# An attention and MLP kernel in float16: 20 more identity matmuls in two waits of TensorE in the first batch

## The chip, the cores and the metric

The kernel runs on one core of one Trainium2 chip. A core has five engines with a queue of instructions each: TensorE (PE, whose weight loads are shown as PEld), VectorE (DVE), ScalarE (ACT), GpSimd (POOL) and SyncE (SP). They run side by side and wait for each other on semaphores. DMA transfers are issued by SP, ACT and POOL and carried out by 16 DMA engines. The metric is the time of one execution in microseconds (us) on the device, taken as the median of several runs.

## The reference

Two layers, one after the other. The first is attention of 12 heads over 448 tokens with a head size of 64, for a batch of 8, with a normalisation of q and k. The second is an MLP of 768 to 3072 to 768 with a normalisation ahead of it and a sum behind.

```python
def rmsnorm(x, g):
    return x / np.sqrt(np.mean(x * x, axis=-1, keepdims=True) + 1e-06) * g
q_n, k_n = rmsnorm(q, g_q), rmsnorm(k, g_k)                 # [8, 12, 448, 64]
scores = 1.0 / np.sqrt(64) * np.matmul(q_n, k_n.transpose(0, 1, 3, 2))
attn = np.exp(scores - np.max(scores, axis=-1, keepdims=True))
attn = attn / (np.sum(attn, axis=-1, keepdims=True) + 1e-09)
x = np.matmul(attn, v).transpose(0, 2, 1, 3).reshape(8, 448, 768)
mu, var = mean and variance of x over the last axis
xn = (x - mu) / np.sqrt(var + 1e-06) * g_ln
out = x + np.maximum(xn @ w_ch1, 0.0) @ w_ch2               # float32
```

The identity matmuls that this case is about are no part of it: nothing reads what they write.

## The kernel before

**How the work is cut.** The heads are taken in pairs, six for each batch, 48 in all. A pair's tokens are seven groups of 128 rows. Pairs are prepared in units of one or two. The MLP of a batch runs while the attention of the next batch is worked on, piece by piece between its matmuls. The last batch's MLP has nothing beside it.

**The order is written out by hand.** Every engine runs its instructions in the order in which the program emits them. For the first batch the list `ORDER` (L39 to L50) gives that order, token by token, and `first_attention` (L502) turns each token into instructions. Those that matter here:

- `Sp.i`: the scores of pair p, group i (L406), one or two matmuls of 448 columns on PE (L417, or L427 and L428 for the left group 6), then an exponential on ACT (L433).
- `Kp`, `Qp`: the transposes of k and q of a pair on PE (L377, L380, L397), with a copy from PSUM behind them: k by DVE (L385), q by ACT for the pairs in `ACT_Q` (0, 2, 4, 5; L400) and otherwise by DVE (L402).
- `mu`: the second copy of q in float16 that the transposes read (L336), for unit 1 on DVE.
- `Vp.i`: exponentials times v (L470, L472).
- `Hn`: n matmuls of the 128 x 128 identity with itself into a PSUM bank of their own, psW, which nothing reads (L541 to L544). Each is one weight load and one matmul.
- `Jn`: the same as transposes, into an unused part of the bank for transposes (L547).
- `Ln`: the loads of a unit of q, k, v by SP (L149, L157).

In the list, `Q0` (transposes of q of the first pair) is followed, with entries for other engines between, by `S0.0`; and `S0.6` is followed by `Q1`.

**The end.** In the last batch the second group of MLP rows ends as follows. PE computes the products of L832, the last of them in two halves of 192 columns. DVE adds each to the sums (L768). SP and ACT store the rows as they are done: L967 for tokens of a batch (tile x), L970 for the left tokens (tile xl), where for each 64 rows of xl SP issues one store and ACT the other. Behind the last product PE runs `END_WORK`, 44 more identity matmuls into psW (L1003). Then each engine loads a flag (L1232) and jumps by it (L1233): a general path, a long piece of program for inputs out of range, is passed over. Behind the jump SP waits for all stores, and the engines meet (L1260).

The few lines of the end that a sentence doesn't say:

```python
for c in range(0, HCOL, 192):
    for s in range(4):
        yield half / 4, lambda s=s, c=c: product(f"4{c}", A2(hi), T4, s, c=slice(c, c + 192))
    yield 0, lambda c=c: self.add(b, t0 + 1, 0, bank[f"4{c}"][:, c:c + 192], c, c + 192)
    yield 0, lambda c=c: self.store(b, t0 + 1, slice(c, c + 192), nc.scalar)
```

Of the kernel before, what the change touches and what calls it, by code (L numbers as in the profile page):

```python
# [36 lines left out]


ORDER = """  # L39
b0 H12 a0 L4 c0 i0 e0 j0 H24 b1 gq0 d0 k0 l0 a1 m0 K0 G gk0 i1 H10 L5 c1 Q0 d1 j1 S0.0 b2 S0.1  # L40
H5 a2 e1 g1 S0.2 c2 S0.3 k1 l1 z0 d2 e2 m1 K1 S0.4 i2 H16 S0.5 S0.6 Q1 g2 H5 J8 b3 l2 j2 k2 c3
V0.0 S1.0 z2 S1.1 S1.2 V1.0 J8 a3 m2 H4 V0.1 z3 S1.3 K2 S1.4 V0.2 Q2 V0.3 V0.4 d3 S1.5 V0.5 V0.6
S2.0 S1.6 V1.1 V1.2 S2.1 e3 W0 i3 K3 V2.0 S2.2 V2.1 S2.3 Q3 j3 T0 S2.4 k3 V1.3 g3 V1.4 S2.5 S2.6
l3 b4 V1.5 m3 c4 S3.0 S3.1 V2.2 S3.2 K4 a4 V1.6 S3.3 V2.3 S3.4 Q4 d4 V2.4 V2.5 V3.0 V3.1 V3.2
V2.6 i4 S3.5 j4 J4 S3.6 V3.3 T1 K5 e4 k4 S4.0 W1 S4.1 S4.2 Q5 z4 b5 S4.3 V3.4 V4.0 V3.5 S4.4
V4.1 V4.2 S4.5 W2 V4.3 S5.0 g4 V3.6 S4.6 S5.1 J4 V5.0 V4.4 G2 S5.2 l4 T3 K6 V4.5 V5.1 V4.6 S5.3
T4 V5.2 a5 L6 V5.3 S5.4 m4 Q6 i5 S5.5 V5.4 S5.6 V5.5 V5.6 T5 S6.0 S6.1 J4 S6.2 A V6.0 S6.3 V6.1
N0 N1 S6.4 S6.5 J4 V6.2 X0 V6.3 d5 j5 N2 S6.6 V6.4 X1 z5 Q7 c5 V6.5 R U0 e5 U1 g5 X2 V6.6 M k5
U2 K7 b6 L7 a6 L8k c6 i6 l5 m5 e6
""".split()  # L50
DMA_UNIT = 7
PE_SET = (DMA_UNIT + 1) % 2
# [1212 lines left out]
```

## Time and profile before

| what | us |
|---|---|
| median of 3 runs | 579.8 (579.79 to 580.12) |
| the profiled execution | 579.4 |
| its span, first to last instruction | 577.9 |
| PE busy | 562.0 (97%) |
| DVE, ACT, POOL busy | 385.5, 363.6, 210.1 |
| first matmul of the MLP (L956, psU) | starts at 51.4 |
| last product of L832 | starts at 570.5 |

The profile is of one execution. Times in it count from the first instruction, so what lies around the span (1.5 us here) isn't in it. A row of the timeline is a start, a duration, an engine, a line of the kernel, the operation with its tiles, and the count of like instructions merged into it; in brackets stands the time for which the engine sat idle before it, and who ended that. A row of a group has smallest, median and largest duration in ns. SPq, ACTq, POOLq and PEldq are what the engines' sequencers do: issues of DMA, semaphores and branches. Queue q1 carries SP's DMAs, q0 those of POOL, q10 those of ACT; q8 and q14 carry instructions. A row of a queue has packets, MB, and the share of 16 DMA engines over the window.

### The profile page before, as it was taken

The page shows a single profiled execution, that of the slowest core. Times are in us where ns is not written, and L with a number is a line of the kernel's source. Part 1 is how long each engine was busy: PE and PEld are TensorE (multiplying, and loading weights), DVE is VectorE, ACT ScalarE, POOL GpSimd, SP SyncE. Part 2 cuts the span into 40 slices and gives each one's busy share as a digit, 9 for nine tenths or more (in the row PEclk, how much of TensorE's full clock was granted, in tenths as well). Part 3 has the DMA queues.
Part 4 walks back from the last instruction along what each step waited for, and adds up shares of the span by engine and source line. Part 5 has one row for each costly group of instructions (what it writes and reads, how often), then busy time and mean ns, then how long its engine had stood idle before and what let it go on. Part 6 is the DMA issues. An engine that isn't in the chain of part 4 may idle for free.

```text
span 577.9 us, 13760 instructions
## 1 busy us (share of the span) xinstructions
PE 562.0 (97%) x5490; PEld 414.9 (72%) x5490; DVE 385.5 (67%) x832; ACT 363.6 (63%) x672; POOL 210.1 (36%) x226
## 2 busy tenths in 40 slices
PE   6788999999999999999999999999999999999998
PEld 4556666687686867777677868777687777777785
DVE  6989577799757686846667586855757643663424
ACT  5998886457674779467675688547776477323130
POOL 4885845404630721554340620654242500020000
PEclk9999999999999999999999999999999999999999
DMA  8999999966773966968673887959643590040202
GB/s 206 259 237 224 220 205 162 184 185 98 133 132 94 140 140 143 133 131 113 124 121 56 175 140 135 122 146 132 126 60 59 133 99 1 9 102 2 83 2 58
DMA packets 175321, 72.59 MB, mean 126 GB/s; under 512 B 138292, under 2 KB 170212, under 8 KB 175252
## 3 DMA queue, kind: packets, MB, share of 16 engines
q1 hardware_dynamic: 134304, 52.75, 44.2%
q0 software_dynamic: 40352, 18.50, 25.0%
q8 instruction: 44, 0.72, 0.5%
q10 hardware_dynamic: 596, 0.41, 0.3%
q14 instruction: 25, 0.20, 0.1%
HBM read 52.76 MB, written 11.01 MB: 110 GB/s over the span
## 4 chain that ended last, share of the span: by engine, by line
PE 90%; DMA 5%; DVE 2%; SPq 2%; issue 0%; ACTq 0%
PE psH L809 34%; PE psP L832 30%; PE psS L417 8%; PE oA L470 5%; PE psC L740 4%; PE psH L730 4%; DMA k<-in_k_dram 2%; PE psS L423 2%; PE oB L472 2%; SPq L157 1%; DMA hS<-in_k_dram 1%; DMA w<-in_v_dram 1%; DMA w2s<-in_q_dram 1%; DMA w2s<-in_k_dram 0%; PE psW L1003 0%
## 5 line engine op out<-in xcount | busy, mean ns | idle before, releaser
L433 ACT ACTIVATE E<-psS,rr_all 128x448 f16<-128x448 f32 x336 | 204.2, 634 | 48.6 <-PE psS L417 40.5
L809 PE MATMUL psH<-xnT,w 128*128 128x256 f16 (+1 forms) x2016 | 225.7, 261 | 0.0
L809 PEld LDWEIGHTS <-w 128*128 128x128 f16 x2016 | 172.8, 98 | 24.4 <-issue 5.0
L812 ACT ACTIVATE hS<-psH 128x512 f16<-128x512 f32 x150 | 89.8, 599 | 97.6 <-PE psH L809 93.2
L832 PEld LDWEIGHTS <-hS 128*128 128x128 f16 x1080 | 100.0, 98 | 57.4 <-issue 1.1
L832 PE MATMUL psP<-w,hS 128*128 128x384 f16 x672 | 127.0, 326 | 0.0
L417 PE MATMUL psS<-qU,kU 128*128 128x448 f16 x288 | 100.9, 352 | 4.7 <-ACT E L433 2.9
L470 PEld LDWEIGHTS <-E 128*128 128x128 f16 x1008 | 70.3, 98 | 35.6 <-issue 2.8
L283 POOL TENSOR_TENSOR k<-k,gprod 128x896 f32<-128x896 f32 x18 | 39.3, 2181 | 138.8 <-ACT khl L263 100.2
L815 DVE TENSOR_TENSOR hS<-hS 128x512 f16<-128x512 f16 (+1 forms) x119 | 58.2, 496 | 19.3 <-ACT hS L812 17.8
L832 PE MATMUL psP<-w2s,hS 128*128 128x384 f16 (+1 forms) x408 | 69.9, 321 | 0.0
L470 PE MATMUL oA<-v,E 128*128 128x65 f16 x864 | 66.8, 193 | 1.1 <-ACT E L433 0.6
L768 DVE SCALAR_TENSOR_TENSOR x<-psP,rs_all,x 128x384 f32<-128x384 f32 x60 | 36.4, 616 | 41.1 <-PE psP L832 40.5
L472 PE MATMUL oB<-v,E 128*128 128x65 f16 x288 | 51.9, 193 | 0.1
L843 POOL TENSOR_TENSOR x<-x,hS 128x384 f32<-128x384 f32 x21 | 23.4, 1127 | 75.2 <-ACT hS L911 74.6
L485 DVE RECIPROCAL rec_all<-oA 128x6 f32<-128x6 f32 x48 | 9.2, 192 | 52.6 <-PE oA L470 52.5
L220 POOL DMA_DIRECT2D v<-in_v_dram x54 | 41.5, 779 | 4.4 <-PE oB L472 3.3
L417 PEld LDWEIGHTS <-kU 128*128 128x128 f16 x288 | 28.1, 98 | 11.1 <-issue 2.2
L911 ACT ACTIVATE hS<-hS,rs_all 128x384 f32<-128x384 f32 x27 | 14.6, 604 | 33.0 <-DVE hS L815 33.0
L472 PEld LDWEIGHTS <-E 128*128 128x128 f16 x336 | 32.4, 97 | 0.3 <-DVE xl L492 0.2
L86 DVE SCALAR_TENSOR_TENSOR qn<-q,rr_all 128x256 f16<-128x256 f32 (+2 forms) x69 | 25.0, 423 | 7.1 <-ACT rr_all L273 7.0
L269 DVE TENSOR_REDUCE ssq<-khl 128x14 f32<-128x896 f32 (+1 forms) x24 | 25.5, 1061 | 3.7 <-ACT khl L263 3.6
(145 smaller groups left out, 626.6 us busy)
## 6 DMA issues: line engine op xcount, KB each, us to landing
k<-in_k_dram SPq DMA_DIRECT2D x19, 384.0 KB, 4.6
q<-in_q_dram SPq DMA_DIRECT2D x18, 384.0 KB, 4.2
out_dram<-x SPq DMA_DIRECT2D x14, 384.0 KB, 3.2
w<-in_moe_w_ch_dram POOLq DMA_DIRECT2D x3, 1536.0 KB, 14.1
w<-in_moe_w_ch_dram POOLq DMA_DIRECT2D x4, 1152.0 KB, 14.6
v<-in_v_dram POOLq DMA_DIRECT2D x54, 64.0 KB, 4.5
out_dram<-x POOLq DMA_DIRECT2D x9, 384.0 KB, 2.7
qU<-qn SPq DMA_TRANSPOSE x90, 3.1
```

The source lines that it names most:

```text
L220: nc.gpsimd.dma_start(out[:, :, j, 0:D], main[:, :, j])
L269: nc.vector.tensor_reduce(out=c["ssq"][:, n], in_=c["sq", n], axis=AX.X, op=ALU.add)
L283: (nc.vector if u in DVE_KG else nc.gpsimd).tensor_tensor(out=c["t"][1], in0=c["t"][1], in1=sh.gprod.unsqueeze(1).broadcast_to([128, g, D] ...
L417: nc.tensor.matmul(ps[0][:, 0:S], c["main"][:, ts(i, 128)], c["q"][:, ts(h, S)], start=True, stop=True)
L433: nc.scalar.activation(out=o, in_=x[:, 0:S], func=AFT.Exp, scale=self.units[u][3][:, g:g + 1], bias=EXP_BIAS)
L470: nc.tensor.matmul(oA[:, t, cs], E[:, ts(t, 128)], rhs, start=(i == 0 and t == 0), stop=(i == 6 and t == 2))
L472: nc.tensor.matmul(oB[:, cs], E[:, 320:448], rhs, start=(i == 0), stop=(i == 6))
L768: self.nc.vector.scalar_tensor_tensor(out=x, in0=ps, scalar=self.rs[:, b, t:t + 1], in1=x, op0=ALU.mult, op1=ALU.add)
L809: nc.tensor.matmul(ps[:, i], sh.w1[:, dc, ts(f + i, 128)], self.xnT[:, dc, 256 - N:256], start=(i == 0 and dc == 0), stop=(i == k - 1 and ...
L812: nc.scalar.activation(out=hT[:, f:f + k], in_=ps, func=AFT.Relu)
L815: nc.vector.tensor_tensor(out=out, in0=a, in1=c, op=op)
L832: nc.tensor.matmul(bank[x][:, c], a[:, f], w[:, f, c], start=(start and f == 0), stop=(stop and f == HALF - 1))
```

## The change

Two tokens are put into `ORDER`: `H8` between `j1` and `S0.0`, and `H12` between `S0.6` and `Q1`. That is 8 more identity matmuls ahead of the first scores, and 12 more ahead of the transposes of the second pair's q. The rest of the list is the same; its lines are broken in other places. On PE these are 20 matmuls and 20 weight loads, 40 instructions, at about the 130th and the 200th of some 11,000. No other engine gets or loses an instruction.

```diff
-b0 H12 a0 L4 c0 i0 e0 j0 H24 b1 gq0 d0 k0 l0 a1 m0 K0 G gk0 i1 H10 L5 c1 Q0 d1 j1 S0.0 b2 S0.1
-H5 a2 e1 g1 S0.2 c2 S0.3 k1 l1 z0 d2 e2 m1 K1 S0.4 i2 H16 S0.5 S0.6 Q1 g2 H5 J8 b3 l2 j2 k2 c3
...
+b0 H12 a0 L4 c0 i0 e0 j0 H24 b1 gq0 d0 k0 l0 a1 m0 K0 G gk0 i1 H10 L5 c1 Q0 d1 j1 H8 S0.0 b2
+S0.1 H5 a2 e1 g1 S0.2 c2 S0.3 k1 l1 z0 d2 e2 m1 K1 S0.4 i2 H16 S0.5 S0.6 H12 Q1 g2 H5 J8 b3 l2
...
```

More of the change, by code (lines that the diff above doesn't have):

```diff
@@ L39 @@
 ORDER = """
-b0 H12 a0 L4 c0 i0 e0 j0 H24 b1 gq0 d0 k0 l0 a1 m0 K0 G gk0 i1 H10 L5 c1 Q0 d1 j1 S0.0 b2 S0.1
-H5 a2 e1 g1 S0.2 c2 S0.3 k1 l1 z0 d2 e2 m1 K1 S0.4 i2 H16 S0.5 S0.6 Q1 g2 H5 J8 b3 l2 j2 k2 c3
[L42 to L49, printed above, removed]
+b0 H12 a0 L4 c0 i0 e0 j0 H24 b1 gq0 d0 k0 l0 a1 m0 K0 G gk0 i1 H10 L5 c1 Q0 d1 j1 H8 S0.0 b2
+S0.1 H5 a2 e1 g1 S0.2 c2 S0.3 k1 l1 z0 d2 e2 m1 K1 S0.4 i2 H16 S0.5 S0.6 H12 Q1 g2 H5 J8 b3 l2
+j2 k2 c3 V0.0 S1.0 z2 S1.1 S1.2 V1.0 J8 a3 m2 H4 V0.1 z3 S1.3 K2 S1.4 V0.2 Q2 V0.3 V0.4 d3 S1.5
+V0.5 V0.6 S2.0 S1.6 V1.1 V1.2 S2.1 e3 W0 i3 K3 V2.0 S2.2 V2.1 S2.3 Q3 j3 T0 S2.4 k3 V1.3 g3 V1.4
+S2.5 S2.6 l3 b4 V1.5 m3 c4 S3.0 S3.1 V2.2 S3.2 K4 a4 V1.6 S3.3 V2.3 S3.4 Q4 d4 V2.4 V2.5 V3.0
+V3.1 V3.2 V2.6 i4 S3.5 j4 J4 S3.6 V3.3 T1 K5 e4 k4 S4.0 W1 S4.1 S4.2 Q5 z4 b5 S4.3 V3.4 V4.0
+V3.5 S4.4 V4.1 V4.2 S4.5 W2 V4.3 S5.0 g4 V3.6 S4.6 S5.1 J4 V5.0 V4.4 G2 S5.2 l4 T3 K6 V4.5 V5.1
+V4.6 S5.3 T4 V5.2 a5 L6 V5.3 S5.4 m4 Q6 i5 S5.5 V5.4 S5.6 V5.5 V5.6 T5 S6.0 S6.1 J4 S6.2 A V6.0
+S6.3 V6.1 N0 N1 S6.4 S6.5 J4 V6.2 X0 V6.3 d5 j5 N2 S6.6 V6.4 X1 z5 Q7 c5 V6.5 R U0 e5 U1 g5 X2
+V6.6 M k5 U2 K7 b6 L7 a6 L8k c6 i6 l5 m5 e6
 """.split()
```

## The prediction

> **What bounds the kernel now.** I read the page first: how full TensorE (PE) is, and how its instructions come in.
>
> ```profile
> span 577.9 us, 13760 instructions
> ...
> PE 562.0 (97%) x5490; PEld 414.9 (72%) x5490; DVE 385.5 (67%) x832; ACT 363.6 (63%) x672; POOL 210.1 (36%) x226
> ...
> PE   6788999999999999999999999999999999999998
> ...
> q8 instruction: 44, 0.72, 0.5%
> ```
>
> PE is busy in tenths of 9 in every slice but the first four and the last, so the time is made in three stretches: a start of about 55 us with holes, a full middle, and an end. The last row says that programs reach an engine as data too: 44 packets of 16.4 KB. PE has 5490 matmuls and as many weight loads, 10,980 instructions; 10,980 by 44 is one packet for each 250 of them or so. So q8 is PE's program, and a fetch is due each time that PE has taken about 250 instructions. I keep that for the end.
>
> Then the chain of waits in order of time, for the start:
>
> ```profile
> 27.80 5.25 SPq L157
> 34.20 6.24 DMA k<-in_k_dram
> 48.45 1.16 DVE xn L674 x3
> 54.61 1.17 PE psU L956 x18
> ```
>
> Up to 54.6 us what ends last is loads, SP's issuing of them, and then VectorE (DVE). PE comes on to the road at 54.6. So the start is not PE's. The rows around the two places where the change puts its matmuls, first PE's and then those of the engines that it waits for (start, duration, in brackets the wait):
>
> ```profile
> 5.88 2.74 PE L544 MATMUL psW<-id 128*128 128x128 f16 x24
> ...
> 10.24 0.56 PE L397 MATMUL psQ<-id,qn 128*128 128x128 f16 x7
> ...
> 11.80 0.54 PE L417 MATMUL psS<-qU,kU 128*128 128x448 f16 x2 [0.99 <-DVE ssq L269]
> ...
> 14.73 1.06 PE L544 MATMUL psW<-id 128*128 128x128 f16 x16
> ...
> 18.12 0.56 PE L397 MATMUL psQ<-id,qn 128*128 128x128 f16 x7 [1.42 <-DVE qn L336]
> ```
>
> ```profile
> 10.85 0.91 ACT L400 COPY qU<-psQ 128x896 f16<-128x896 f16 x1 [0.99 <-PE psQ L397]
> ...
> 17.16 0.90 DVE L336 COPY qn<-qn 128x448 f16<-128x448 f16 x1
> ```
>
> S0.0 starts at 11.80, after ScalarE's copy of qU (to 11.76); Q1 starts at 18.12, after DVE's copy of qn (to 18.06). Both starts are set by other engines.
>
> Now the end, by engine: PE's matmuls, DVE's last sums, SP's issues of stores.
>
> ```profile
> 568.50 2.11 PE L832 MATMUL psP<-w,hS 128*128 128x384 f16 x12
> 570.45 2.14 PE L832 MATMUL psP<-w2s,hS 128*128 128x192 f16 x24
> 572.43 2.62 PE L1003 MATMUL psW<-id 128*128 128x128 f16 x44
> ```
>
> ```profile
> 571.64 0.42 DVE L768 SCALAR_TENSOR_TENSOR xl<-psP,rs_all,xl 128x192 f32<-128x192 f32 x1
> 572.63 0.42 DVE L768 SCALAR_TENSOR_TENSOR xl<-psP,rs_all,xl 128x192 f32<-128x192 f32 x1 [0.57 <-PE psP L832]
> ```
>
> ```profile
> 570.35 0.55 SPq L970 DMA_DIRECT2D out_dram<-xl  x1
> 571.60 1.59 SPq L967 DMA_DIRECT2D out_dram<-x  x1
> 573.28 1.22 SPq L970 DMA_DIRECT2D out_dram<-xl  x2
> ```
>
> ```profile
> L967 SPq DMA_DIRECT2D out_dram<-x x16: 332/495/1586, 117.7 to 571.6; - x16
> ```
>
> The last product is summed at 572.63 + 0.42 = 573.05, and SP could issue the last store then. But SP spends 1.59 us on the issue at 571.60, where the same line takes 0.50 in the median of 16 and 0.33 at least. It begins the pair at 573.28, and the second of them only at about 573.9. What fell on that issue shows in q8: first a window of 0.1 us from 571.2, then, for two like cases, SP and q8 in the window of 506 to 508, and SP at 17 us:
>
> ```profile
> q8 instruction: 1, 0.02, 98.9%
> ```
>
> ```profile
> 506.48 1.20 SPq L967 DMA_DIRECT2D out_dram<-x  x1
> ```
>
> ```profile
> q8 instruction: 1, 0.02, 3.1%
> ```
>
> ```profile
> 16.97 0.95 SPq L149 DMA_DIRECT2D hS<-in_q_dram  x1
> ```
>
> 98.9% of 16 engines over 0.1 us is 1.58 us: a fetch of PE's program, which the slices of that window (2.5 ns each, the bytes in the 17th) put at 571.24 to 572.82. SP's issue ends at 573.19, 0.37 us behind it. At 506 us a fetch of 3.1% x 16 x 2 us = 0.99 us lies at the same line, and the issue takes 1.20 instead of 0.50; the issue at 16.97, in a stretch that holds one fetch too, takes 0.95. So **an SP issue that meets a fetch of PE's program ends only when the fetch has ended**. What sets the end:
>
> ```profile
> SPq L1260 <- DMA out_dram<-xl: 1.0, 1, 1.0
> ```
>
> ```profile
> L1260 SPq EVENT_SEMAPHORE  x14: 17/28/28, 575.1 to 577.8; - x14
> ...
> L1260 SPq DRAIN  x3: 7/7/13, 577.0 to 577.3; - x3
> ...
> L1260 PEldq DRAIN x2: 8/8/8, 575.5 to 577.4; - x2
> ```
>
> PE is through at 575.5. SP, which waits for the stores, stands 1.0 us for a store of xl and drains at 577.0; then the engines meet, and the span ends at 577.9. The end is the last stores, not PE.
>
> **The change part by part.** (1) H8 ahead of S0.0: 8 matmuls. At 14.73 sixteen take (1.06 - 0.22) / 15 = 0.056 us each; earlier, 24 take (2.74 - 0.30) / 23 = 0.106. The transposes of Q0 end at 10.80, so H8 needs 0.45 to 0.85 of a wait of 0.99: nothing. (2) H12 ahead of Q1: 0.67 (1.27 at the slow rate) of a wait of 1.42: nothing. Cover gone, both together would cost 20 x 0.056 = 1.1 us. Nothing waits for them, they read the identity and write a bank that the other H write, no other engine's work is changed. A gain in the start is excluded too, as PE isn't on the road there.
>
> (3) 40 instructions more ahead of everything that follows: 20 matmuls and their 20 weight loads. Each later fetch is due 40 instructions earlier in the work: 20 matmuls. For the last fetch these are matmuls of L832: of 384 columns (2.11 - 0.33) / 11 = 0.162 us each, of 192 columns (2.14 - 0.22) / 23 = 0.083. So it comes between 20 x 0.083 = 1.7 and 20 x 0.162 = 3.2 us earlier, at 568.0 to 569.6. It takes 1.0 (506 us) to 1.6, and ends by 571.2 at the latest, ahead of the issue at 571.60. It can at worst meet the first stores at 570.35, which have 1.2 us until SP is needed again.
>
> What that gives: x is issued 571.60 to 572.1; the first xl half is summed at 572.06 and issued then; the second, summed at 573.05, is issued at 573.09 instead of 573.9 (half the pair's 1.22 behind 573.28): 0.8 us earlier. How soon it lands:
>
> ```profile
> DMA to landing us min/median/max: 4.0/4.0/4.0
> DMA to landing us min/median/max: 2.3/2.6/2.7
> DMA to landing us min/median/max: 2.3/2.3/2.3
> DMA to landing us min/median/max: 2.8/2.8/2.8
> ```
>
> These are x at 571.60; x at its line from 510 to 560 us, undisturbed; and ScalarE's two small stores of xl, at 572.1 and at 573.08. x lands 4.0 - 2.6 = 1.4 us sooner after its issue, so that its 0.4 MB are out of the way of the small ones. The last store of SP now lands at about 576.9 (the drain at 577.0 follows it), 3.0 after its issue. Then: 573.09 + 2.3 = 575.4 at best, 573.09 + 3.0 = 576.1 at worst. The gain is 0.8 to 1.5. PE's drain at 575.5 is the floor: 1.5 earlier than SP's. I take the middle between 2.3 and 2.8, so 575.65, and a gain of 1.2.
>
> Fetches in the middle move too, but PE is full there and doesn't wait for SP. In the start there are three; cost and gain of a moved one lie between -0.95 (the stretched issue at 16.97 off the road altogether) and +1.1 (1.59 - 0.50 again), on a road that has SP on it: I take 0, as SP there stands for landings and full queues anyway (5.25 us at 27.80).
>
> The sum: 577.9 - 1.2 = 576.7 of span. The profiled execution took 579.4, so 578.2 for its like; the median of the runs shown is 579.8, 0.4 above it, and from that the **forecast is 578.6 us**.
>
> A rule speaks against this. The Trainium skill, "Runtime: NRT & Kernel Launch", section "Instruction fetch mechanics", says that the program is streamed in blocks of 256 instructions and that crossing a block's boundary is mostly hidden; by it the sum would be 579.8. The rows above differ from it in one place: the fetch is hidden from PE, not from SP's issue of 1.59 us.
>
> **The rivals.** *Nothing*: the moved fetch frees SP, but the last store lands when it did, because something else holds it, or the fetch's place is not set by the count of instructions. For it: only three stretched issues are shown here. Against: the issue ends 0.37 us behind the fetch, and x lands 1.4 us late. Then the gain is 0 and the time 579.8. It is what the skill's rule on crossings, above, comes to.
>
> *The start pays*: the fetches before 54.6 us move on to SP issues that are on the road. One costs up to 1.1; two, less the end's gain, 2.2 - 1.2 = +1.0: 580.8. It decides when a load's issue at 15 to 42 us is stretched without a wait behind it to take it up. Against: SP waits behind most of them.
>
> *The jump at the end*, on the slower side. PE's program ends in a jump over the general path:
>
> ```profile
> L1233 PEldq COMPARE_BRANCH  x1: 487/487/487, 574.8 to 574.8; - x1
> ...
> L1233 PEldq EVENT_SEMAPHORE  x1: 51/51/51, 575.4 to 575.4; - x1
> ```
>
> ```profile
> q8 instruction: 1, 0.02, 5.4%
> ```
>
> PE goes on 0.1 us after it, so the code behind the jump is there; only then comes one more fetch, 5.4% x 16 x 1.4 us = 1.2 us long, landing at about 577.2. If 40 instructions more put that code outside what is loaded, PE has to wait from 575.3 to 577.2, and drains at 577.45, 0.45 behind SP now: 580.3; two fetches in a row, 1.9 more: 582.2, which I take. It decides if a boundary of a block falls between the fetch at 571.2 and the jump. Against: from 571.2 to the jump PE takes about 88 (the 44 of L1003) plus a few tens; 40 more stay under 250. The same section of the skill says that a taken branch to code that isn't loaded stalls for a fetch; no run here shows one.
>
> **How the numbers follow.** Forecast 0.72: with 1.16 us or more gained (0.2%, about what a measurement of this kernel can tell from no change) 0.52, with less 0.20. Nothing 0.12. The start 0.09, of it 0.07 slower and 0.02 within. The jump 0.07. Faster 0.52; same 0.20 + 0.12 + 0.02 = 0.34; slower 0.07 + 0.07 = 0.14. The range goes from a gain of 1.6 (the bound and a tenth) to the rival with nothing and 0.3 more, the spread of the runs shown: 578.2 to 580.1.
>
> **What would show it.** In the profile after: L417 at 11.8 and L397 at 18.1 as before, 20 more of L544 ahead of them; 44 packets on q8 still; no packet of q8 from 571 to 573, one between 568.0 and 571.2; SP's issue at 571.6 at 0.33 to 0.6 us; SP's drain between 575.6 and 576.3; PE's branch at 574.8 as now. I am wrong if SP's issue is short and the drain still comes at 577.0, if the start's end moves from 54.6, or if PE's event behind the branch comes 1 us or more after it.

## The result and the profile after

| | before | after |
|---|---|---|
| median, 21 runs each (us) | 579.84 | 578.46 |
| lowest | 578.58 | 577.96 |
| profiled execution, its span (us) | 579.4, 577.9 | 578.2, 576.7 |

The ratio is 0.9977, with an interval of 0.9970 to 0.9984: 1.4 us faster (0.9 to 1.7). One run of before, at 593.1 us, was slow and isn't in the ratio. The forecast was 578.6.

First the page, the same rows as before:

```profile
span 576.7 us, 13800 instructions
...
PE 563.6 (98%) x5510; PEld 416.5 (72%) x5510; DVE 385.5 (67%) x832; ACT 363.4 (63%) x672; POOL 210.0 (36%) x226
...
q8 instruction: 44, 0.72, 0.5%
```

PE has 20 matmuls and 20 weight loads more and is busy 1.6 us longer; the span is 1.2 us shorter. So the gain isn't work that went away. The 44 packets of PE's program are still 44.

The start, in the timeline. First the identity matmuls that stand ahead of everything that was changed:

```profile
6.32 2.74 PE L544 MATMUL psW<-id 128*128 128x128 f16 x24
```

Then the two places, first PE's rows (the new matmuls are the x8 and the x12 of L544), then those of the engines that PE waits for:

```profile
10.80 0.74 PE L397 MATMUL psQ<-id,qn 128*128 128x128 f16 x7
11.37 0.61 PE L544 MATMUL psW<-id 128*128 128x128 f16 x8
12.53 0.54 PE L417 MATMUL psS<-qU,kU 128*128 128x448 f16 x2 [0.55 <-ACT qU L400]
...
17.26 0.83 PE L544 MATMUL psW<-id 128*128 128x128 f16 x12
18.56 0.56 PE L397 MATMUL psQ<-id,qn 128*128 128x128 f16 x7 [0.47 <-DVE qn L336]
```

```profile
11.57 0.91 ACT L400 COPY qU<-psQ 128x896 f16<-128x896 f16 x1 [1.81 <-PE psQ L397]
...
17.60 0.91 DVE L336 COPY qn<-qn 128x448 f16<-128x448 f16 x1
```

H8 is through at 11.98, and PE waits on for 0.55 until ScalarE's copy is done (11.57 + 0.91 = 12.48). H12 is through at 18.09 and PE waits on for 0.47 until DVE's copy is done (18.51). The matmuls lie inside the waits. S0.0 starts 0.73 and Q1 0.44 later than in the profile of before, but the 24 matmuls at 6.32, ahead of the change, started 0.44 later too, and Q0, which stands ahead of H8, ends another 0.3 later (10.80 + 0.74 = 11.54, where it was 10.80): that is this execution, not the change.

The end, by the same three views as before. PE:

```profile
568.92 2.11 PE L832 MATMUL psP<-w,hS 128*128 128x384 f16 x12
570.87 2.14 PE L832 MATMUL psP<-w2s,hS 128*128 128x192 f16 x24
572.85 2.62 PE L1003 MATMUL psW<-id 128*128 128x128 f16 x44
```

DVE, and SP's issues of stores:

```profile
572.06 0.42 DVE L768 SCALAR_TENSOR_TENSOR xl<-psP,rs_all,xl 128x192 f32<-128x192 f32 x1
573.05 0.42 DVE L768 SCALAR_TENSOR_TENSOR xl<-psP,rs_all,xl 128x192 f32<-128x192 f32 x1 [0.57 <-PE psP L832]
```

```profile
570.76 0.55 SPq L970 DMA_DIRECT2D out_dram<-xl  x1
572.01 0.34 SPq L967 DMA_DIRECT2D out_dram<-x  x1
572.51 1.46 SPq L970 DMA_DIRECT2D out_dram<-xl  x2
```

The issue of x takes 0.34 us where it took 1.59. The last fetch of PE's program, in the DMA view from 568 to 570 (40 slices of 0.05 us; its bytes are in the eighth):

```profile
GB/s 0 0 0 0 0 0 0 328 0 0 0 0 0 0 0 0 0 0 0 0 0 0 0 0 0 0 0 0 0 0 0 0 0 0 0 0 0 0 0 0
...
q8 instruction: 1, 0.02, 3.7%
```

It lies at 568.36 and takes 3.7% x 16 x 2 us = 1.2 us, to 569.55, ahead of SP's four stores of the end. How long x took to land, then what SP stood for behind the jump, and the drains:

```profile
out_dram<-x SPq DMA_DIRECT2D x1, 384.0 KB, 2.4
```

```profile
SPq L1260 <- DMA out_dram<-xl: 0.5, 1, 0.5
```

```profile
L1260 SPq EVENT_SEMAPHORE  x14: 17/28/28, 574.6 to 576.6; - x14
...
L1260 SPq DRAIN  x3: 7/7/13, 575.8 to 576.1; - x3
...
L1260 PEldq DRAIN  x2: 8/8/8, 575.7 to 576.2; - x2
```

x lands 2.4 us after its issue where it took 4.0; SP stands 0.5 us for the last store of xl where it stood 1.0; it drains at 575.8 where it drained at 577.0, and the span ends at 576.7.

Below I count the end from the start of the last halves of L832 (the row of 192 columns, x24), because the start of an execution varies. From there to the end of the span it was 577.86 - 570.45 = 7.4 us before and is 576.68 - 570.87 = 5.8 after. From the 24 matmuls ahead of the change to the last halves it was 570.45 - 5.88 = 564.57 before and is 570.87 - 6.32 = 564.55 after: the whole middle is as long as it was, to 0.02 us. In the profiles of the other versions below it is within 0.25 us of this, but for two that are named there. All that changed lies in the last 7 us.

### The profile page after: what moved, and what is told of

Read it like the earlier page. It is cut to its first block, busy times and chain, and to the rows that moved or that the text cites. A ratio compares the mean times of both kernels' runs of the same rounds, so it can differ in the third digit from the quotient of the medians.

```text
span 576.7 us, 13800 instructions
## 1 busy us (share of the span) xinstructions
PE 563.6 (98%) x5510; PEld 416.5 (72%) x5510; DVE 385.5 (67%) x832; ACT 363.4 (63%) x672; POOL 210.0 (36%) x226
## 4 chain that ended last, share of the span: by engine, by line
PE 92%; DVE 3%; ACT 3%; issue 1%; DMA 0%; ACTq 0%; DVEq 0%
PE psH L809 34%; PE psP L832 30%; PE psS L417 8%; PE oA L470 5%; PE psC L740 4%; PE psH L730 4%; ACT E L433 2%; PE oB L472 2%; PE psS L423 2%; DVE ssq L269 1%; PE psW L544 1%; PE tr L380 1%; ACT qU L400 0%; PE psW L1003 0%; DMA w<-in_g_k_dram 0%
## 5 line engine op out<-in xcount | busy, mean ns | idle before, releaser
L832 PEld LDWEIGHTS <-hS 128*128 128x128 f16 x1080 | 100.0, 98 | 57.4 <-issue 1.1
L832 PE MATMUL psP<-w,hS 128*128 128x384 f16 x672 | 127.0, 326 | 0.0
L832 PE MATMUL psP<-w2s,hS 128*128 128x384 f16 (+1 forms) x408 | 69.9, 322 | 0.0
L843 POOL TENSOR_TENSOR x<-x,hS 128x384 f32<-128x384 f32 x21 | 23.4, 1126 | 75.3 <-ACT hS L911 74.6
```

Source lines behind the costliest of these rows:

```text
L832: nc.tensor.matmul(bank[x][:, c], a[:, f], w[:, f, c], start=(start and f == 0), stop=(stop and f == HALF - 1))
```

## The experiments

The theory: the moved fetch makes the gain, and the filled waits give nothing. The first rival: the filled waits themselves bring it (PE's work behind them is quicker, or the start is). Others are the three rivals of the prediction. The table has the kernels that tell of the count and the place of PE's instructions; times in us from the start of the last halves, the fetches read as above. Fetch, issue and end are of one execution each. Each ratio is to runs of the kernel before in the same rounds as that version; but for the row of after, its medians there were 579.3 to 579.4, 0.4 to 0.6 below that of the result.

| kernel | PE instructions, against before | ratio to before (95%) | last fetch, from and to | issue of x | end of the span |
|---|---|---|---|---|---|
| before | 0 | | 0.79 to 2.37 | 1.59 | 7.40 |
| before, another look | 0 | | 0.94 to 1.99 | 0.34 | 6.00 |
| waits filled, count kept | 0 | 1.0001 (0.9990 to 1.0012) | 0.71 to 1.70 | 0.86 | 6.20 |
| 4 matmuls | +8 | 0.9982 (0.9972 to 0.9991) | 0.19 to 1.49 | 0.73 | 6.09 |
| H8 alone | +16 | 0.9985 (0.9975 to 0.9995) | -0.63 to 0.54 | 0.34 | 5.80 |
| H12 alone | +24 | 0.9983 (0.9975 to 0.9992) | -1.22 to -0.28 | 0.34 | 5.85 |
| after (H8 and H12) | +40 | 0.9977 (0.9970 to 0.9984) | -2.51 to -1.32 | 0.34 | 5.81 |
| 20 in another place | +40 | 1.0001 (0.9991 to 1.0010) | -2.39 to -1.45 | 0.34 | 5.80 |
| 20 fewer | -40 | 1.0012 (0.9999 to 1.0025) | 3.69 to 4.63 | 0.34 | 7.27 |

**The waits filled, the count kept.** H8 and H12 are added, and 20 of the like transposes J, which nothing reads, are taken out behind them.

```diff
-...j1 S0.0 b2 ...S0.6 Q1 g2 H5 J8 b3 ...S1.2 V1.0 J8 a3 ...S3.5 j4 J4 S3.6...
+...j1 H8 S0.0 b2 ...S0.6 H12 Q1 g2 H5 b3 ...S1.2 V1.0 a3 ...S3.5 j4 S3.6...
```

> The same 20 identity matmuls in the same two waits, and 20 identity transposes of the first batch taken out (8, 8 and 4), so that PE has as many instructions ahead of the end as before. The theory of the moved fetch: the last packet of q8 ahead of the jump lies at 571 to 573 us again, SP's issue of the last x store takes 1.2 to 1.7 us, and the time is that of before, 579.8 (ratio 0.999 to 1.001). The rival that the filled waits themselves gave the gain: 578.5 (ratio 0.998).

Measured: 579.3 us, ratio 1.0001. The gain is gone. SP's issues, and the fetch in the window 571.5 to 573 (slices of 0.0375 us, its bytes in the sixth, so 571.71):

```profile
570.89 0.55 SPq L970 DMA_DIRECT2D out_dram<-xl  x1
572.14 0.86 SPq L967 DMA_DIRECT2D out_dram<-x  x1
573.11 1.19 SPq L970 DMA_DIRECT2D out_dram<-xl  x2
```

```profile
GB/s 0 0 0 0 0 437 0 0 0 0 0 0 0 0 0 246 82 164 246 287 123 123 369 82 41 246 246 123 41 451 287 328 369 369 410 205 42 123 41 0
...
q8 instruction: 1, 0.02, 4.1%
```

The fetch is back where it was from the last halves (0.71 instead of 0.79), and the issue of x is held again, to 573.00, 0.3 us behind the fetch's end at 572.69. It is held less than in the profile of before, mostly since this fetch takes 0.98 us and not 1.58.

**One part alone, and less.** H8 alone; H12 alone; then only four matmuls (`H4` ahead of `Q1`).

```diff
-...j1 S0.0 b2 S0.1
+...j1 H8 S0.0 b2 S0.1
```
```diff
-...S0.5 S0.6 Q1 g2
+...S0.5 S0.6 H12 Q1 g2
```
```diff
-...S0.5 S0.6 Q1 g2
+...S0.5 S0.6 H4 Q1 g2
```

> Only the 8 matmuls ahead of S0.0: 16 instructions more instead of 40. The theory of the moved fetch: 8 matmuls of 0.162 us, so the packet of q8 comes 1.3 us earlier than in before, at about 570, ends by 571.6, may stretch SP's first store at 570.3 but not the x store, and nearly the whole gain is there: 578.5 to 579.0. The rival that the filled waits gave it: the part of 8 in 20, 579.2 to 579.4.

> Only the 12 matmuls ahead of Q1: 24 instructions more instead of 40. The theory of the moved fetch: the packet of q8 comes 12 x 0.162 = 1.9 us earlier than in before, at about 569.3, clear of the x store: 578.5, the whole gain. The rival that the filled waits gave it: the part of 12 in 20, about 579.0.

> Only 4 identity matmuls ahead of Q1: 8 instructions more. The theory of the moved fetch: the packet of q8 comes 0.65 us earlier than in before, at about 570.6, and is over by 571.6 if it takes 1.0 and by 572.2 if it takes 1.6: SP's x issue is held for 0.3 to 0.9 us, and the time lies between before and 8 matmuls (ratio 0.9985), at 0.9985 to 0.9995. The rival that the gain goes with the filled waits: the part of 4 in 20, 0.9995.

Measured: 0.9985, 0.9983 and 0.9982, that is 0.9, 1.0 and 1.0 us, each interval overlapping that of the full change. The gain doesn't grow with what is filled. (A share of 8 or 12 in 20 would be 0.9991 or 0.9986, which these intervals still hold; the share of 4, 0.9995, lies outside the interval of the four.) What grows is the distance of the fetch: against before it comes 0.6, 1.4, 2.0 and 3.3 us earlier for 4, 8, 12 and 20 matmuls, 0.15 to 0.18 us for each, and a matmul of 384 columns in L832 takes 0.16. With four matmuls the fetch still lies on the issue of x (0.73 us); why the median gains as much as the others there, the one profile doesn't show. It is of an execution of 578.7 us, where seven of the ten took 578.1 to 578.4, so it may not be the usual case.

**The same count in another place.** 20 transposes into the unused part, at a place late in the first batch where PE is full.

```diff
-U2 K7 b6 L7 ...
+U2 J20 K7 b6 L7 ...
```

> No matmuls in the two waits; 20 identity transposes at about 55 us instead, where PE is full, so 40 more instructions ahead of the end at a cost on PE's road of 20 x 0.056 = 1.1 us. The theory of the moved fetch: the last packet of q8 comes 3.2 us earlier as seen from the last products, SP's x issue takes 0.3 to 0.6, the end is 1.2 to 1.6 us shorter, and the time is 579.8 + 1.1 - 1.4 = 579.5. The rival that the filled waits gave it: 579.8 + 1.1 = 580.9, with the x issue at 1.2 us or more.

Measured: 579.3, ratio 1.0001. This is neither a loss of 1.1 nor a gain of 1.4. Its profile has both: SP's issue of x, then the two rows of PE that bound the middle, with the 20 transposes between them.

```profile
573.50 0.34 SPq L967 DMA_DIRECT2D out_dram<-x  x1
```

```profile
6.73 2.74 PE L544 MATMUL psW<-id 128*128 128x128 f16 x24
...
56.44 1.28 PE L547 MATMUL tr<-id 128*128 128x128 f16 x20
...
572.37 2.14 PE L832 MATMUL psP<-w2s,hS 128*128 128x192 f16 x24
```

The middle is 572.37 - 6.73 = 565.64 us, 1.1 more than before, which is 20 x 0.056, the rate of such matmuls in the start. The chain of what ended last runs through the 20 transposes:

```profile
56.61 1.12 PE tr L547 x20
```

In a full PE they are paid. The end is 5.80, as short as after the change. So the count shortens the end from this place too, and the waits only let PE have the matmuls at no price.

**20 fewer.** The same 20 transposes taken out, and nothing added.

```diff
-...H5 J8 b3 ...V1.0 J8 a3 ...j4 J4 S3.6...
+...H5 b3 ...V1.0 a3 ...j4 S3.6...
```

> 20 identity transposes of the first batch taken out and nothing put in: 40 instructions fewer ahead of the end. The theory of the moved fetch: the packet of q8 comes 1.5 to 2 us later than in before, at about 572.9; SP's x issue is short (0.3 to 0.6) and it is the last store's issue at 573.1 that is stretched, to 1.0 us or more, so that it ends at 574.3 to 574.8 instead of 574.5: 579.3 to 580.2, about as before. The rival that the place of the fetch does not matter: SP's issues as in before, x at 1.6 us, 579.8.

Measured: 580.2, ratio 1.0012. The fetch came at 575.20, well behind what I had expected (572.9; 20 matmuls of the end are 1.7 us, and it moved by 2.9). No issue of SP was held, and the end is 7.27 all the same. PE's jump and what comes behind it:

```profile
L1233 PEldq COMPARE_BRANCH  x1: 1927/1927/1927, 575.7 to 575.7; - x1
...
L1233 PEldq EVENT_SEMAPHORE  x1: 51/51/51, 577.6 to 577.6; - x1
```

```profile
L1260 SPq DRAIN  x3: 7/7/13, 577.9 to 578.2; - x3
```

The jump takes 1.93 us instead of 0.39 to 0.49: PE goes on at 577.6, 1.5 us after the fetch has landed. This is the jump rival, not in the change but in the opposite one. It isn't shown to set this end alone, though: the same fetch lies among the data of the last stores, whose last write is at 577.02, 5.5 from the last halves where it is 4.4 after the change, and SP drains at 577.9, just behind PE (577.8). Either would end the kernel here. Nor is the count all that changed: the granted clock of PE is 0.50 from 20.0 to 23.4 us in this profile, about where 16 of the 20 transposes stood (18.8 and 20.8 us in before), and 1.00 there in before. Six of the twelve runs show a mean clock of 0.997, with a median of 580.6 against 579.9 for the other six; of the 35 runs of before in these rounds, six show one below 1. (With the count kept, where the same transposes are out but 20 matmuls stand ahead of them, the clock is 1.00 there, and one run of twelve is below 1.) So the ratio of this version isn't that of the count alone.

**x issued by ScalarE.** The kernel before, with the last big store moved to the other queue of the end.

```diff
-(nc.gpsimd if eng is nc.gpsimd else nc.sync).dma_start(out[b, 0:384]...
+(nc.sync if eng is None else eng).dma_start(out[b, 0:384]...
```

> The kernel before, with the last x store issued by ScalarE instead of SP; the fetch stays where it was. The theory that the fetch holds SP's issue: SP is free for its two small stores, at 572.1 and 573.1, and if ScalarE's issue is not held (its small one at 572.1 took 0.47 us beside the fetch) the time is 578.6 to 579.0. If any issue of the large store is held by a fetch, ScalarE's takes 1.5 us, its own small stores are late, and the time is 579.5 to 580. The rival that the landing, not the issue, was slow: 579.8 with short issues.

Measured: 579.3, ratio 0.9996 (0.9985 to 1.0007): no gain. The fetch is at 571.57 to 572.65. ScalarE's issues, then SP's:

```profile
570.60 0.55 ACTq L970 DMA_DIRECT2D out_dram<-xl  x1
571.85 1.16 ACTq L967 DMA_DIRECT2D out_dram<-x  x1
573.11 1.17 ACTq L970 DMA_DIRECT2D out_dram<-xl  x2
```

```profile
570.59 3.20 SPq L970 DMA_DIRECT2D out_dram<-xl  x3
```

Now it is ScalarE's issue of x that is held, to 573.01, 0.36 us behind the fetch, and its small stores are late. SP's two small issues, in the single records, take 0.50 and 0.47 us and are on time. So the hold isn't SP's own: it came to the queue that carries x.

**A shorter end for PE.** `END_WORK` 4 instead of 44, in the kernel after and in the kernel before; then 24 in the kernel after.

```diff
-END_WORK = 44
+END_WORK = 4
```

> The changed kernel with 4 instead of 44 identity matmuls behind the last product. PE's drain now is at 575.7, SP's at 575.8: if SP's stores alone set the end, the time stays 578.5 within 0.2; if PE's tail takes part, up to 0.3 less. The jump comes 80 instructions sooner, but the fetch is in by 569.6, so PE's event behind the branch still comes within 0.2 us; if the code behind the jump is not there, PE stalls 1 to 2 us at the branch.

> The kernel before with 4 instead of 44 identity matmuls behind the last product: the jump comes about 2.2 us earlier, at 572.6, while the fetch at 571.2 to 572.8 is still under way. The rival of the jump in the prediction, tried: PE's branch then takes 1 us or more instead of 0.5, but drains by 575.5 and costs nothing, 579.6 to 580.0. If the fetch is not due any more before the jump, SP's x issue is short and the time is 578.6 to 579.2.

> The changed kernel with 24 identity matmuls behind the last product. With 4 of them the fetch behind PE's jump came at 573.9 us, lay on the data of the last stores, and the gain was lost. The theory that it is this second fetch: with 24 the jump comes 20 x 0.056 = 1.1 us sooner than with 44, the second fetch at about 575.1 by the clock of the changed kernel's profile, where the last data are written at 575.26: half the loss or less, 578.4 to 579.0. The rival that it is the shortened program itself (another place of the jump in its block): the loss is there in full, 579.5, or not at all, wherever the second fetch lies.

Measured: the kernel after with 4 takes 579.5, ratio to before 1.0006 (0.9997 to 1.0016): its gain is lost, where 578.5 was expected. With 24 it takes 578.4, 0.9984 (0.9975 to 0.9993): kept, at the lower edge of the 578.4 to 579.0 expected. The kernel before with 4 takes 580.1, 1.0012 (1.0002 to 1.0021): a little slower, where no cost was expected. In the first the last fetch is early (-2.39) and SP's issues are all short. But behind the jump comes one more fetch, and with PE through earlier it comes earlier. The window from 573.8 to 575 of that kernel (slices of 0.03 us, the packet in the third), and its drains:

```profile
GB/s 128 128 700 128 154 205 231 359 231 308 205 129 154 77 51 26 0 51 77 102 179 154 128 256 102 231 103 154 154 129 205 205 230 179 205 154 26 325 51 273
...
q8 instruction: 1, 0.02, 5.2%
```

```profile
L1260 SPq DRAIN  x3: 7/7/13, 576.6 to 577.0; - x3
...
L1260 PEldq DRAIN  x2: 8/8/8, 573.1 to 577.0; - x2
```

It lies from 573.88 to 574.88 among the last stores (the last issue is at 573.22), and SP drains 3.5 us after PE; the end is 6.94 instead of 5.81. No issue is held: the data alone are late. With 24, the fetch behind the jump lies at 574.74, 0.1 us behind the last write (574.63), and the end is 5.80. That is where the theory of the second fetch has no loss, but the rival (the jump at another place in the program) also allows for no loss with 24, so this run doesn't part the two; what speaks for the fetch is where it lies in the run with 4. In the kernel before with 4 the jump itself meets a fetch (571.71 to 573.07) that isn't in yet:

```profile
L1233 PEldq COMPARE_BRANCH  x1: 1887/1887/1887, 572.6 to 572.6; - x1
```

The jump takes 1.89 us; PE goes on at 574.6, 1.5 us behind the landing, as with 20 fewer, but here SP is later than PE still. Its x passes in 0.34, and in the single records the issue behind it takes 0.90, to 573.48, 0.4 behind the fetch. This execution, at 578.6, was the fastest of twelve, 1.5 us below their median, so it doesn't show what makes the others slower.

**The kernel before, one more look.**

> The kernel before, unchanged, for a second profile. If the start moves by itself from execution to execution, the last product's start differs from 570.45 by some tenths of a us, as it does between the profiles of before and of the changed kernel (0.42). The theory of the moved fetch: the last packet of q8 ahead of the jump again comes 0.8 us behind the start of the last halves of 192 columns, and SP's x issue is held to 0.3 to 0.4 us behind its end.

Measured in this one run: 578.7, an end of 6.00. SP's issues:

```profile
571.05 0.55 SPq L970 DMA_DIRECT2D out_dram<-xl  x1
572.30 0.34 SPq L967 DMA_DIRECT2D out_dram<-x  x1
572.80 1.45 SPq L970 DMA_DIRECT2D out_dram<-xl  x2
```

The fetch is at 572.10 to 573.15, and x, issued 0.2 us after its start, passes in 0.34. The next issue is held instead: in the single records the first of the pair takes 0.73 us, to 573.52, 0.38 behind the fetch; the second waits for its sum in any case and is on time. I had expected x to be held. Its data are late even so:

```profile
DMA to landing us min/median/max: 3.1/3.1/3.1
```

That is 3.1 us from issue to landing where it is 2.4 after the change; before with a short end, where x passes too, it is 3.3. So a fetch that meets x delays its data whether or not the issue is held, and the runs don't part the two costs. A fetch at about the same place costs 0.2 us of end here, 0.4 with the count kept, and 1.6 in the profile of before, each against the 5.80 of a fetch out of the way.

The kept traces hold more such cases than these ends. In the 13 profiles, 20 issues of x (L967, by SP or ScalarE) begin while a fetch is under way. 17 of them take 0.73 to 1.69 us and end 0.2 to 0.4 us after the fetch; two take 0.34 (this one and the one before with a short end); the last began only 0.1 us ahead of the fetch's end.

No version beat the kernel after; four, eight or twelve of the matmuls, or an end of 24, can't be told from it.

## Why the prediction was right, point by point

- **Steps 1 and 2, the waits filled at no cost and for no gain:** right. PE still waits 0.55 and 0.47 us behind the new matmuls for the copies named, and the same fill with the count kept gives 1.0001.
- **Step 3, the last fetch 1.7 to 3.2 us earlier:** 3.3 us, just past the upper bound; all 20 matmuls count at the price of the 384-column ones. Since the fetch of before begins 0.79 us into the halves of 192 columns, some 9 of the 20 should have counted at 0.083, which makes about 2.5 us; why they don't is open.
- **The issue of x at 0.33 to 0.50 and the last issue 0.8 earlier:** 0.34, and the last at 573.50, which less the 0.42 us by which the last halves start later is 573.08 on the clock of before; 573.09 was forecast.
- **Its landing 2.3 to 3.0 us after the issue, SP's drain between 575.6 and 576.3:** the drain is at 575.8, 2.3 us after that issue. On the clock of before that is 575.4, 1.6 us earlier than the 577.0 there; the bounds were 0.8 to 1.5, and 1.2 was taken. The issue gave 0.8 of it, as forecast, and the landing 0.8 (3.1 to 2.3 us) where 0.4 was taken. That the span is 576.7, as forecast, is luck: the end is 1.6 shorter, and this execution reached it 0.4 later.
- **The start at 0:** right to 0.02 us between the two profiles, the middle included.
- **The size:** 1.4 us in the medians against 1.2. The profile of before that gave the terms was a dear case, one in which the fetch cost much: its end is 7.40 us, and another look at the same kernel shows 6.00. So the mechanism was right, and that the size came out so near is in part luck. How often each case comes stays open.
- **"An SP issue that meets a fetch of PE's program ends only when the fetch has ended"** was too strict. An issue on ScalarE is held as well; small stores beside it pass; and twice x passed and the next one was held. What held in all six cases at the end (three with x on SP, one on ScalarE, two with the issue behind x) is that the held issue was on the queue that carries x and ended 0.3 to 0.4 us after the fetch. What chooses between x and the one behind it stays open.
- **The rival Nothing** fell: the gain follows the fetch. The rule that it rests on (the Trainium skill, "Runtime: NRT & Kernel Launch", "Instruction fetch mechanics": a crossing is mostly hidden) agrees with PE's own rows here (from 55 to 573 us, with 40 of the 44 fetches, the profile of before lists no wait of PE), not with the stores: 0.9 to 1.7 us of the kernel's time.
- **The start pays** fell: the 564.55 us up to the last halves are as long as the 564.57 before.
- **The jump at the end** didn't come, since the code behind the jump was loaded, as argued: the branch takes 0.39 us. With 20 fewer, and before with a short end, PE did wait there, 1.9 us. That fits the stall that the same section of the Trainium skill states for a taken branch whose target isn't loaded; which code the fetch ahead of it held, no view here shows.

## What to carry to other kernels

When a kernel ends in stores, look where the last packet of PE's program lies beside them: filler instructions can matter by their number, which moves that packet, and not by the wait that they fill. To tell the two apart, keep the fill and take as many like instructions out elsewhere, then add the same number at another place. An instruction count tuned in this way holds for this program alone: a few instructions more or fewer anywhere ahead move the fetch again.

## What the runs showed that I had not expected

- The fetch behind the jump can cost as much as the one ahead of it when PE is through too early: 1.1 us of end with an `END_WORK` of 4, nothing with 24 or 44 in the kernel after. The 44 identity matmuls at the end of PE's program, which nothing waits for, keep that fetch behind the last write.
- PE's branch took 1.89 and 1.93 us when the last fetch wasn't in, and went on only 1.5 us after the packet had landed.
- With 20 fewer the last fetch moved by 2.9 us where 20 matmuls of the end are 1.7. Why isn't known. The middle of that kernel came 0.9 us longer (571.50 - 6.07 = 565.43), although it holds less work. The granted clock of 0.50 from 20.0 to 23.4 us goes with it: half of the runs of this version show a lower mean clock. Whether that makes all of the 0.9 us, no run shows.
